# Four unused tiles in SBUF that shift where TensorE's operands begin

## The chip, the cores and the metric

The kernel runs on one core of one Trainium2 chip. The metric is device time in microseconds, taken over one execution of the whole program; the median of several runs is given. PE is TensorE, DVE VectorE, ACT ScalarE, POOL GpSimd, SP the queue that issues the DMAs.

## The reference

An attention layer over 12480 tokens of 128 channels with 32 inducing points, then two feed-forward layers of width 2048. Cut to what matters:

```python
def mab(q, kv):
    s = scale * (q @ kv.transpose(0, 2, 1))
    a = np.exp(s - s.max(-1, keepdims=True))
    a /= a.sum(-1, keepdims=True) + 1e-09
    return a @ kv
h = mab(I, x)                              # 32 inducing points look at all tokens
x = mab(x, h)                              # all tokens look at the 32 results
x = (s * np.maximum(x @ w_in, 0) ** 2 + b) @ w_out
y = x @ w_in2
g = np.where(y >= 1, y, np.where(y <= -1, 0.0, (y + 1) ** 2 / 4))
return g @ w_out2
```

## The kernel before

The tokens are cut into 25 blocks of 512 (the last has 192). A first stage of some 50 us loads x in seven groups of blocks, transposes the blocks on PE (L301), keeps a running softmax for the inducing points (L318, L363, L374) and ends with hT. A second stage starts the feed-forward work while the weights are still being turned into the form in which they are used; there the second matrix of the first layer is multiplied as plain fp32 (`out1_whole`, L721), and each of these matmuls stands in the trace as two records.

From about 125 us on the work goes in steps. A step is two chunks of 128 hidden units of one block, eight steps are a block, and each step does four things on PE, 20 matmuls with 512 columns each, all of type fp32r: two matmuls of the first layer's input side (L656, in1), six of the second layer's output side (L709 to L711, out2), six of the second layer's input side (L746 to L748, in2) and six of the first layer's output side (L709 to L711 again, out1). The six are three products for each of two chunks, since weights and activations are each split into a high part and a rest (hi, lo) to keep the accuracy of fp32. The stages of one step belong to different blocks: the second layer runs 18 steps behind the first. Between the matmuls ACT does relu, squares and one of the two casts, POOL the split behind the first layer (L235, L686), DVE the clip, the sum and the other rest (L753, L764, L774). The order of the steady part is written out in a list (ORDER), that of the start and the end comes from a planner with a table of durations. None of this uses addresses.

Addresses come from pools. A pool lays its tiles one behind the other in each of the 128 partitions. From the left of the memory come `keep` (ident, hT and five columns of one element, each taking 32 bytes), `xts` (x, later also y and cl), `homes` (six halves of the weights of 8192 bytes each, before that the loaded blocks xc), and then `pre` for the first stage, whose place is taken over by `wk` (g1, qin, hw, qt) at the `switch` of L541. From the right come `cv` (the weights being converted, win, wo_s), whose place is later taken over by `wk2` (hi, lo, o). The tile y of a block is held in a place of `xts`, hi and lo in `wk2`, the weights in `homes`. Because of the five small columns on the left, and of where the right side begins, all of the tiles that the matmuls of a step read begin 32 bytes beside a multiple of 64 in the built program. The starts in bytes of a partition, and their rest by 2048:

| tile | read by | before | rest | after | rest |
|---|---|---|---|---|---|
| x, y (first) | L746 to L748 | 17696 | 1312 | 18432 | 0 |
| halves (first) | weights of L709 to L711, L746 to L748 | 67616 | 32 | 69632 | 0 |
| qt | L656 | 143968 | 608 | 147456 | 0 |
| hw | weights of L656 | 141920 | 608 | 145408 | 0 |
| hi, lo (first) | L709 to L711 | 188384 | 2016 | 186368 | 0 |
| g1 | L721 | 117344 | 608 | 120832 | 0 |
| wo_s | weights of L721 | 182240 | 2016 | 180224 | 0 |

Of the kernel before, what the change touches and what calls it, by code (L numbers as in the profile page):

```python
# [10 lines left out]
F32 = mybir.dt.float32  # L11
# [85 lines left out]
def tb(bl):  # L97
    return TB if bl < NB - 1 else TBL
# [73 lines left out]
def moe_attn_kernel(ctx: ExitStack, tc: tile.TileContext, x, ind, w_in, w_out, s, b, w_in2, w_out2, out):  # L172
# [6 lines left out]
    def kt(shape, name, dt=F32):  # L179
        return keep.tile(shape, dt, tag=name, name=name)  # L180

    ident = kt([128, 128], "ident")
    xts = ctx.enter_context(tc.tile_pool(name="xts", bufs=1, reuse_waits="tile"))
    xT = []
    while len(xT) < NB:
        i = len(xT)
        pair = i in PAIRS
        t = xts.tile([C, 1 + pair, tb(i)], F32, tag=f"x{i}", name=f"x{i}")
        xT += [t[:, k, :] for k in range(1 + pair)]
    hT = kt([C, 4 * NM], "hT")  # L190
    bcol = kt([C, 1], "bcol")
    s_sb = kt([128, 1], "s_sb")
    b_sb = kt([128, 1], "b_sb")
    mhalf = kt([128, 1], "mhalf")
    mneg = kt([128, 1], "mneg")

    flat = lambda t: t.rearrange("p f d -> p (f d)")

# [9 lines left out]
        return halves[name, k]  # L208

    cx, px = ExitStack(), ExitStack()  # L210
    cv = cx.enter_context(tc.tile_pool(name="cv", bufs=1, side="right"))
    pb = cx.enter_context(tc.tile_pool(name="pb", bufs=1, space=PSUM, side="right"))
    pre = px.enter_context(tc.tile_pool(name="pre", bufs=1))
# [325 lines left out]
    pool = {}  # L539

    def switch():  # L541
        px.close()
        pool["wk"] = ctx.enter_context(tc.tile_pool(name="wk", bufs=1, reuse_waits="tile"))
        pool["pm"] = ctx.enter_context(tc.tile_pool(name="pm", bufs=1, space=PSUM, reuse_waits="tile"))

    def finish():
        t = add("PE", 0.12, f_pm, P["top", NG - 1], P["xT", NB - 1])
        t = add("DVE", 0.6, f_gm, t)
        t = add("PE", 0.05, f_pg, t)
        t = add("DVE", 0.13, f_w, t)  # L550
        tw = add("ACT", 0.1, lambda: nc.scalar.activation(w_, w_, AF.Exp, scale=scale), t)
        weighted(NG - 1)
        t = add("DVE", 0.07, lambda: nc.vector.tensor_mul(lsum, lsum, w_), tw, P["lsum", NG - 1])
        t = add("PE", 0.05, f_pl, t)
        t = add("DVE", 0.27, f_ri, t)
        t = add("DVE", 0.26, lambda: nc.vector.tensor_scalar(hsum, hsum, w_, ri, op0=ALU.mult, op1=ALU.mult),
                t, tw, P["hs", NG - 1])
        t = add("PE", 0.22, f_ht, t)
        t = add("DVE", 0.2, lambda: nc.vector.tensor_copy(hT, T.pop("pht")[:, :128]), t)
        P["hT"] = add("switch", 0.01, switch, t)  # L560
# [639 lines left out]
```

## Time and profile before

| | |
|---|---|
| runs | 1002.73, 999.62, 1002.39 us; median 1002.39 |
| profiled execution, span from first to last instruction | 999.5 us |
| PE busy | 977.5 us (98%) |
| ACT, DVE, POOL busy | 845.5, 806.1, 753.8 us |
| DMA, mean over the span | 28 GB/s |

The page of the profile gives busy time by engine and in 40 slices, with the clock that was granted to TensorE; the trace answers with waits (who waited for whom), windows (busy time in a stretch) and a timeline, in which the start of each instruction is read. For PE the starts matter: matmuls are pipelined, so one begins before the one ahead of it has ended, and durations overlap.

### The profile page before, as it was taken

How to read it: one execution, taken by the hardware profiler on the slowest of the kernel's cores; microseconds unless marked ns; L12 is line 12 of the kernel's file. 1: busy time of each engine (PE TensorE's matmuls, PEld its weight loads, DVE VectorE, ACT ScalarE, POOL GpSimd, SP SyncE). 2: the span in 40 equal slices, each digit the busy share in tenths (PEclk: the TensorE clock that was granted, in tenths of full speed). 3: DMA queues.
4: the chain of work that ended last, by engine and by line, in shares of the span. 5: the costliest groups of instructions: out<-in, count | busy, mean ns of one | idle time of the engine just before them, and what ended most of it. 6: DMA issues, size and time to landing. Idle time of an engine off the chain costs nothing.

```text
span 999.5 us, 12391 instructions
## 1 busy us (share of the span) xinstructions
PE 977.5 (98%) x4492; PEld 772.6 (77%) x4492; DVE 806.1 (81%) x834; ACT 845.5 (85%) x910; POOL 753.8 (75%) x510
## 2 busy tenths in 40 slices
PE   5999999999999999999999999999999999999997
PEld 3754588888888888888888888888888888888776
DVE  6868788888888878888788888878878878878895
ACT  5748989889898988998888898998998988898774
POOL 0121379888889888889889888888888888887463
PEclk9979999999999999999999999999999999999999
DMA  8602000100002000002000002000001000000001
GB/s 312 220 27 80 0 1 11 45 9 11 5 6 53 11 1 11 11 1 53 11 1 11 11 0 54 11 1 11 11 1 42 11 1 11 16 1 11 11 12 15
DMA packets 65469, 28.11 MB, mean 28 GB/s; under 512 B 54016, under 2 KB 58368, under 8 KB 65408
## 3 DMA queue, kind: packets, MB, share of 16 engines
q1 hardware_dynamic: 65408, 27.33, 11.2%
q8 instruction: 35, 0.57, 0.2%
q14 instruction: 26, 0.21, 0.1%
HBM read 14.80 MB, written 6.39 MB: 21 GB/s over the span
## 4 chain that ended last, share of the span: by engine, by line
PE 94%; DVE 2%; ACT 2%; DMA 1%; issue 0%; SPq 0%; ACTq 0%
PE y L709 17%; PE y L710 17%; PE y L711 17%; PE h L746 9%; PE h L748 9%; PE h L747 9%; PE h L656 9%; PE y L721 3%; PE ptr L301 1%; DMA xc<-in_x_dram 1%; ACT g L676 1%; DVE cl L753 1%; PE ph L374 1%; ACT g L669 1%; DVE lo L774 1%; PE pw L878 1%
## 5 line engine op out<-in xcount | busy, mean ns | idle before, releaser
L686 POOL TENSOR_TENSOR lo<-g,hi 128x1024 fp32r<-128x1024 f32 (+1 forms) x182 | 427.8, 2351 | 15.2
L753 DVE TENSOR_SCALAR cl<-h 128x1024 f32<-128x1024 f32 (+2 forms) x202 | 239.5, 1187 | 141.9 <-PE h L748 141.7
L757 ACT ACTIVATE cl<-cl,mhalf 128x1024 f32<-128x1024 f32 (+2 forms) x202 | 227.0, 1125 | 97.9 <-DVE cl L753 96.5
L709 PE MATMUL y<-hi,wout 128*128 128x512 f32 (+1 forms) x748 | 293.0, 392 | 0.9 <-DVE o L799 0.9
L710 PE MATMUL y<-lo,wout 128*128 128x512 f32 (+1 forms) x748 | 293.0, 392 | 0.0
L711 PE MATMUL y<-hi,wout 128*128 128x512 f32 (+1 forms) x748 | 292.8, 391 | 0.0
L235 POOL TENSOR_SCALAR hi<-g 128x1024 fp32r<-128x1024 f32 (+1 forms) x182 | 186.4, 1024 | 103.3 <-PE y L711 86.4
L764 DVE SCALAR_TENSOR_TENSOR h<-h,cl 128x1024 f32<-128x1024 f32 x182 | 223.4, 1227 | 14.0 <-ACT cl L757 2.7
L774 DVE TENSOR_TENSOR lo<-h,hi 128x1024 fp32r<-128x1024 f32 x182 | 221.3, 1216 | 1.2 <-ACT hi L231 0.5
L676 ACT ACTIVATE g<-g 128x1024 f32<-128x1024 f32 (+1 forms) x200 | 207.5, 1039 | 5.4
L669 ACT ACTIVATE g<-h 128x1024 f32<-128x1024 f32 (+1 forms) x197 | 194.3, 986 | 5.3 <-PE h L656 5.3
L231 ACT CAST hi<-h 128x1024 fp32r<-128x1024 f32 x182 | 181.8, 999 | 4.8 <-DVE h L764 4.8
L711 PEld LDWEIGHTS y<-hi,wout 128*128 128x128 f32 x748 | 140.6, 188 | 32.1
L710 PEld LDWEIGHTS y<-lo,wout 128*128 128x128 f32 x748 | 140.6, 188 | 31.8
L709 PEld LDWEIGHTS y<-hi,wout 128*128 128x128 f32 x748 | 140.6, 188 | 30.8 <-issue 1.3
L746 PE MATMUL h<-y,win 128*128 128x512 f32 (+1 forms) x400 | 156.2, 390 | 1.1 <-DVE lo L774 1.0
L748 PE MATMUL h<-y,win 128*128 128x512 f32 (+1 forms) x400 | 155.9, 390 | 0.0
L747 PE MATMUL h<-y,win 128*128 128x512 f32 (+1 forms) x400 | 153.7, 384 | 0.0
L656 PE MATMUL h<-qt,hw 128*128 128x512 f32 (+1 forms) x400 | 125.3, 397 | 0.7 <-ACT g L669 0.6
L656 PEld LDWEIGHTS h<-qt,hw 128*128 128x128 f32 x400 | 74.4, 188 | 24.1 <-issue 6.2
L746 PEld LDWEIGHTS h<-y,win 128*128 128x128 f32 x400 | 75.1, 188 | 19.8 <-DVE lo L774 2.0
L747 PEld LDWEIGHTS h<-y,win 128*128 128x128 f32 x400 | 75.2, 188 | 17.1
(139 smaller groups left out, 617.3 us busy)
## 6 DMA issues: line engine op xcount, KB each, us to landing
xc<-in_x_dram SPq DMA_DIRECT2D x24, 256.0 KB, 6.8
out_dram<-o SPq DMA_DIRECT2D x96, 64.0 KB, 2.2
qin<-x SPq DMA_DIRECT2D x92, 64.0 KB, 2.0
raw_in<-in_moe_w_in_dram SPq DMA_DIRECT2D x8, 512.0 KB, 5.8
raw_out<-in_moe_w_out_dram SPq DMA_DIRECT2D x8, 512.0 KB, 6.8
xc<-in_x_dram SPq DMA_DIRECT2D x1, 96.0 KB, 6.9
qin<-x SPq DMA_DIRECT2D x4, 24.0 KB, 2.7
out_dram<-o SPq DMA_DIRECT2D x4, 24.0 KB, 1.9
```

The costliest lines, as they stand in the source:

```text
L656: nc.tensor.matmul(p[:, j, :tb(bl)], hw[f // 4][:, (f % 4) * 128:(f % 4 + 1) * 128], qt[bl], start=True, stop=True)
L686: engine[eng].tensor_sub(lo1[t], g1.pop(t), hi1[t].bitcast(F32))
L709: nc.tensor.matmul(p, whi, hi[:, j, :], start=first, stop=False)
L710: nc.tensor.matmul(p, whi, lo[:, j, :], start=False, stop=False)
L711: nc.tensor.matmul(p, wlo, hi[:, j, :], start=False, stop=last)
L746: nc.tensor.matmul(p[:, j, :tb(bl)], whi, y1h[bl], start=True, stop=False)
L747: nc.tensor.matmul(p[:, j, :tb(bl)], wlo, y1h[bl], start=False, stop=False)
L748: nc.tensor.matmul(p[:, j, :tb(bl)], whi, y1l[bl], start=False, stop=True)
L753: nc.vector.tensor_scalar(cl[t][:, part(js)], h2[t][:, part(js), :tb(t // SPB)], -1.0, 1.0, op0=ALU.max, op1=ALU.min)
L757: nc.scalar.activation(k, k, AF.Square, bias=mhalf, scale=0.5)
L764: nc.vector.scalar_tensor_tensor(oo[t][:, part(js)], h, -1.0, cl[t][:, part(js)], op0=ALU.max, op1=ALU.add)
L774: engine[eng].tensor_sub(lo2[t][:, part(js)], oo[t][:, part(js)], hi2[t][:, part(js)].bitcast(F32))
```

## The change

Four tiles are allocated that nothing writes or reads: 736 bytes at the end of `keep`, 1280 bytes at the end of `xts`, 1472 bytes at the start of `wk`, and 2016 bytes at the right edge, in a pool of its own ahead of `cv`. All tiles laid out behind them shift; the table above has the starts before and after. The tiles of `keep` itself stay (ident at 16512, hT at 17024). The smaller tiles of `pre` that lie behind odd sizes (ind_sb, iT, hsum, e, eT and the last block of xc) were at multiples of 64 and are now 32 bytes beside one.

```diff
+    xts.tile([128, 320], F32, tag="xgap", name="xgap")
     hT = kt([C, 4 * NM], "hT")
...
     mneg = kt([128, 1], "mneg")
+    kt([128, 184], "gap")
...
     cx, px = ExitStack(), ExitStack()
+    right = ctx.enter_context(tc.tile_pool(name="right", bufs=1, side="right"))
+    right.tile([128, 504], F32, tag="rgap", name="rgap")
     cv = cx.enter_context(tc.tile_pool(name="cv", bufs=1, side="right"))
...
     def switch():
         px.close()
         pool["wk"] = ctx.enter_context(tc.tile_pool(name="wk", bufs=1, reuse_waits="tile"))
+        pool["wk"].tile([128, 368], F32, tag="wgap", name="wgap")
```

The instructions of all five queues are the same and in the same order. Since `wk` takes over the place of `pre` and the two shift by different amounts, a tile of `wk` may lie on other tiles of `pre` than before, and with that three waits differ, all in the start. On ACT, around 57 to 72 us, where the high parts of the first weights (hh) are cast and the first relus run, before:

```order
L882 CAST hh0_783<-pw0_768 128x512 [waits PE_49]
L882 CAST hh1_794<-pw1_781 128x512 [waits PE_49,Activation_49]
L882 CAST hh2_832<-pw2_823 128x512 [waits PE_49]
L669 ACTIVATE g1_0_844<-h1_0_838 128x1024 [waits PE_49]
L676 ACTIVATE g1_0_844<-g1_0_844 128x1024 [waits Activation_49]
L882 CAST hh3_862<-pw3_854 128x512 [waits PE_49]
L433 ACTIVATE cvs_out21_864<-raw_out21_581 128x512 [waits DMAHW7_49,DVE_49]
L606 ACTIVATE x1_65<-x1_65 128x512 [waits DVE_49]
L669 ACTIVATE g1_1_879<-h1_1_870 128x1024 [waits PE_49]
```

and the same place after the change:

```order
L887 CAST hh0_790<-pw0_775 128x512 [waits PE_49,Activation_49]
L887 CAST hh1_801<-pw1_788 128x512 [waits PE_49]
L887 CAST hh2_839<-pw2_830 128x512 [waits PE_49]
L674 ACTIVATE g1_0_851<-h1_0_845 128x1024 [waits PE_49]
L681 ACTIVATE g1_0_851<-g1_0_851 128x1024 [waits Activation_49]
L887 CAST hh3_869<-pw3_861 128x512 [waits PE_49]
L437 ACTIVATE cvs_out21_871<-raw_out21_587 128x512 [waits DMAHW7_49,DVE_49]
L611 ACTIVATE x1_65<-x1_65 128x512 [waits DVE_49]
L674 ACTIVATE g1_1_886<-h1_1_877 128x1024 [waits DMAHW2_49,PE_49]
```

Nothing moved here; the wait for ACT's own queue goes from hh1 to hh0, and the relu of step 1 waits for a DMA too. The third is on SP, where the first of the four DMAs that fill qin2 waits for PE before and not after.

## Rows read from the trace of the kernel before

**Rows 1.** The page: busy by engine, slices of PE and clock, chain.

```profile
PE 977.5 (98%) x4492; PEld 772.6 (77%) x4492; DVE 806.1 (81%) x834; ACT 845.5 (85%) x910; POOL 753.8 (75%) x510
...
PE   5999999999999999999999999999999999999997
...
PEclk9979999999999999999999999999999999999999
...
PE 94%; DVE 2%; ACT 2%; DMA 1%; issue 0%; SPq 0%; ACTq 0%
```

**Rows 2.** Waits, 125 to 910 us: who <- for whom: us, times, longest.

```profile
DVE cl L753 <- PE h L748: 134.8, 166, 0.9
POOL hi L235 <- PE y L711: 81.7, 94, 1.2
ACT cl L757 <- DVE cl L753: 79.6, 143, 0.6
```

**Rows 3.** Windows of 200 us: busy time by engine, sum and mean.

```profile
400.00:600.00 200.00, 200.00 (x868) 162.59 (x867) 163.08 (x146) 178.91 (x182) 178.19 (x118) 1.00 0.07 12
...
sum 600.00, PE 600.00 PEld 487.75 DVE 489.41 ACT 534.33 POOL 523.99; mean PE 200.00 PEld 162.58 DVE 163.14 ACT 178.11 POOL 174.66
```

**Rows 4.** Timeline of PE: start, duration; steps at 126, 500, 911 us.

```profile
125.72 0.62 PE L656 MATMUL h<-qt,hw 128*128 128x512 f32 x2
...
499.94 0.62 PE L656 MATMUL h<-qt,hw 128*128 128x512 f32 x2
500.39 0.39 PE L709 MATMUL y<-hi,wout 128*128 128x512 f32 x1
...
501.78 0.39 PE L746 MATMUL h<-y,win 128*128 128x512 f32 x1
...
503.16 0.39 PE L709 MATMUL y<-hi,wout 128*128 128x512 f32 x1
503.39 0.40 PE L710 MATMUL y<-lo,wout 128*128 128x512 f32 x1
503.63 0.39 PE L711 MATMUL y<-hi,wout 128*128 128x512 f32 x1
...
504.56 0.62 PE L656 MATMUL h<-qt,hw 128*128 128x512 f32 x2
...
911.12 0.39 PE L656 MATMUL h<-qt,hw 128*128 128x512 f32 x1
```

**Rows 5.** Timeline of PE in the start: third and sixth record of eight.

```profile
89.05 0.59 PE L721 MATMUL y<-g,wo_s 128*128 128x512 f32 x1
...
90.33 0.59 PE L721 MATMUL y<-g,wo_s 128*128 128x512 f32 x1
```

**Rows 6.** Groups of PE by shape: count, busy, mean ns of one.

```profile
L709 PE MATMUL y<-hi,wout 128*128 128x512 f32 x732 | 288.8, 395 | 0.9 <-DVE o L799 0.9
L710 PE MATMUL y<-lo,wout 128*128 128x512 f32 x732 | 288.6, 394 | 0.0
...
L748 PE MATMUL h<-y,win 128*128 128x512 f32 x384 | 151.5, 395 | 0.0
L746 PE MATMUL h<-y,win 128*128 128x512 f32 x384 | 151.5, 395 | 1.1 <-DVE lo L774 1.0
...
L656 PE MATMUL h<-qt,hw 128*128 128x512 f32 x384 | 122.3, 402 | 0.7 <-ACT g L669 0.6
...
L374 PE MATMUL ph<-xc,eT 128*32 128x128 f32 x192 | 6.5, 276 | 0.0
...
L363 PE MATMUL pe<-ident,e 128*128 128x128 f32 x24 | 3.9, 283 | 0.0
```

**Rows 7.** ACT's timeline at 71 us; xc's loads: issue times, time to landing.

```profile
71.18 1.02 ACT L669 ACTIVATE g<-h 128x1024 f32<-128x1024 f32 x1 [0.58 <-PE h L656]
...
L284 SPq DMA_DIRECT2D xc<-in_x_dram x25: 327/328/777, 3.0 to 26.9; - x25
...
xc<-in_x_dram SPq DMA_DIRECT2D x1, 96.0 KB, 6.9
```

## The prediction

> **What bounds the kernel now.** I read the profile from the whole towards the single instruction. First the busy line and the slices [rows 1]: PE is busy for 977.5 of 999.5 us, at nine tenths in all slices but the first and the last, with the granted clock at its upper level of 2.4 GHz almost throughout, and the chain that ended last runs 94% over PE. Then the waits between 125 and 910 us [rows 2]: the longest are DVE's, POOL's and ACT's, DVE and POOL both for matmuls of PE, and no row has PE as the one that waits. So in four fifths of the run nothing that another engine does sets the time. The windows say the same [rows 3]: in 600 us PE is busy for 600.00, ACT for 534.33, POOL for 523.99, DVE for 489.41.
>
> What is left is how fast PE itself streams. A busy PE is not a PE at its peak, so I look at starts, not at durations, which overlap. One steady step is 20 matmuls of 512 columns of fp32r, and it goes from 499.94 to 504.56 us [rows 4]: 4.62 us, or 231.0 ns for a matmul. The same row is at 125.72 and at 911.12 us [rows 4], 785.40 us apart, which is 170 steps of 4.62 us: 3400 matmuls at one pace, whatever the softmax steps, stores and loads in between do. For comparison, the plain fp32 matmuls of the start (L721, two records each): three records take from 89.05 to 90.33 us [rows 5], 0.427 us a record. At 2.4 GHz that is 1024 cycles, two for each of 512 columns, with nothing on top; half of it, 213.3 ns, is the time of 512 columns at one a cycle. An fp32r matmul takes 17.7 ns more, 8%. That excess is the only time in the steady part that a change of addresses could give back.
>
> **The change part by part.** No instruction is added or taken away, and on PE, DVE and POOL the order and the waits are the same as before. Only addresses move, and three waits.
>
> *Excess per matmul.* All tiles that the fp32r matmuls read (qt, hw, hi, lo, y, the halves) start 32 bytes beside a multiple of 64 before and at a multiple of 2048 after. There are 3 x 732 + 4 x 384 = 3732 such matmuls of 512 columns [rows 6]; L711 and L747, not shown there, have as many as their neighbours. The trace of before has none of them with another start, so their price is bounded from both sides. If the whole excess is due to the start, 17.7 ns x 3732 = 66 us go. If none is, nothing goes. Between them: 2048 bytes that begin in the middle of a 64-byte piece touch 33 pieces, not 32; if a matmul took time by pieces it would fall from 231.0 to 224.0 ns, and 7.0 ns x 3732 = 26 us would go. Upward, the largest step that the order of starts shows is 503.39 to 503.63 us [rows 4], about 5 ns over the mean; if all 3400 steady matmuls became so, 17 us would come.
>
> I take zero, by the rows nearest to it. The fp32 records of L721 read g and wo_s, which also start 32 beside a multiple of 64, and show no excess at all [rows 5]; so such a start costs nothing where columns are read at half the pace. That does not exclude a cost at the full pace, but nothing in the trace shows one. Nor does the offset that a tile has within 2048 bytes: within the step, the two matmuls of L656 (moving tile at offset 608) take 0.45 us, the six of L709 to L711 behind them (offset 2016) 1.39 us, the six of L746 to L748 (offset 1312) 1.38 us and the last six 1.40 us [rows 4], that is 225, 232, 230 and 233 ns each. Four places with three offsets lie within 4% and the same offset gives 232 and 233, so I see a pace of fp32r, not a cost of a place.
>
> The Trainium skill, "SBUF — State Buffer", Specifications (TRN2), gives the memory lines of 16 bytes; a start 32 beside a multiple of 64 is the start of such a line as much as one at a multiple of 2048, and by that the sum is zero. No run here shows the line's size.
>
> *Other readers of the moved tiles.* If DVE, ACT or POOL became slower or faster by the move, PE would cover it: the steady step leaves ACT 4.62 - 4.62 x 534.33 / 600 = 0.51 us and POOL 0.59 us [rows 3]. If that cover went (a PE step of 4.27 us, all of the excess gone), ACT would still need only 4.11 us, and so would be late next, but just short of setting the pace.
>
> *Tiles that lose their start.* In the first 50 us, e, eT, hsum, iT and ind_sb go from multiples of 64 to 32 beside one. They are read as fp32, which at that start shows no excess [rows 5]: zero. The most of them are the 192 and 24 of L374 and L363 [rows 6]; if each paid 17.7 ns, 4 us would be added.
>
> *Waits.* ACT's relu into the second g1 buffer (L669) now also waits for the landing of the last xc block, since its buffer lies where that tile was. The last xc load was issued at 26.9 us and took 6.9 us to land [rows 7]; the relu starts at 71.18 us [rows 7]. The wait was over some 37 us before, and nothing queued behind it on ACT is held. A CAST of hh waits for an earlier instruction of ACT's own queue in place of its neighbour, and the first qin2 DMA on SP waits for PE no more; it stands behind qin1 in the same queue, so at most its own short wait goes. All zero.
>
> The sum is zero. The profiled execution's span is 999.5 us, 0.1 below the fastest of the runs shown and 2.9 below their median of 1002.4; zero against the span is zero against the median, and I give 1002.
>
> **The rivals.** *The start does cost at the full pace (faster).* For it: the excess is there, it is the same in all 170 steps, and all tiles of fp32r share the start. Against it: the fp32 records without excess, and that the trace names no cause. Worked out above: 976 us by pieces of 64 bytes, 936 us if all goes. Since ACT's 4.11 us a step stays under PE's 4.27, no other engine takes the gain back in the steady part.
> The Trainium skill, "TensorE: Matmul & The Clock Gate", Back-to-back issue gap, speaks for this rival: it gives a matmul of N columns N / 2.4 + 2.5 ns, 215.8 ns for 512. The steady step disagrees with its 231.0 ns, and if the start were the reason, 15.2 ns x 3732 = 57 us would go, an estimate from that page of 946 us.
>
> *Weights and moving data from the same place (slower).* After the change both of PE's streams begin at multiples of 512 bytes in all matmuls. If the weight load, which runs beside the stream of the matmul before, met it more often, each steady matmul would go to the largest step seen, 5 ns more: 1002 + 17 = 1019 us. It decides from 1 ns a matmul (3.7 us) on. Against it: hw and qt already stand at equal offsets (608, steps of 512), and L656 has the shortest steps of all [rows 4].
>
> *The change doesn't do what it says.* The addresses of the built program do move, so this is left only for the few tiles of the first 50 us named above, at most 4 us.
>
> **How the numbers follow.** No change: 0.50. Faster through the start: 0.38, of which 0.12 for about 976 us or a little above, 0.26 for deeper, down to 936. Slower: 0.12, most of it up to 1019. A measurement of this kernel tells about 0.3% (3 us) from no change. The range goes down to 945, where seven eighths of the excess are gone (58 of 66 us), so that only the lowest part of the faster rival is left out, and up to 1006, the 4 us of the first stage; some 0.15 lies outside. The likeliest case's own range is 999 to 1006.
>
> **What would show it.** Right: the step in the timeline is again 4.62 us, and L721's records 0.427 us. Wrong, faster: the step is 4.48 us or less with PE still at 100% in the windows; if it is 4.27 to 4.35, look whether ACT then shows as the one that PE waits for. Wrong, slower: a step above 4.64 us with the same set of waits. If the step is unchanged and the time is not, the first 120 us or the end have moved, and the waits of ACT and SP in the start are the place to look. What would make the prediction wrong is one thing above all: that fp32r's 8% over one column a cycle is a matter of where a tile begins and not of the type.

## The result and the profile after

The changed kernel takes 986.01 us (median of 4 runs, 984.17 to 987.54); beside it the kernel before took 1002.56 us (999.62 to 1006.63). The ratio is 0.983, with a 95% interval of 0.980 to 0.986: faster by 1.7%. I had forecast no change, so the likeliest case was wrong; the time lies inside the stated range, 945 to 1006 us. The profiled execution took 984.17 us with a span of 982.4 us, 17.1 us less than the span of before.

The page of the changed kernel: busy time by engine, and the chain that ended last.

```profile
PE 959.7 (98%) x4492; PEld 770.0 (78%) x4492; DVE 805.0 (82%) x834; ACT 843.6 (86%) x910; POOL 753.3 (77%) x510
...
PE 93%; ACT 2%; DVE 2%; DMA 2%; issue 0%; DVEq 0%; ACTq 0%
```

Against [rows 1] the counts are the same on every engine. PE's busy time fell by 17.8 us, that of the others by 3 us or less, and the chain still runs over PE. So PE does the same work faster. Where it does shows in its timeline (start, duration): the steps that answer to those of [rows 4], lines moved by five.

```profile
123.89 0.39 PE L661 MATMUL h<-qt,hw 128*128 128x512 f32 x1
...
500.16 0.62 PE L661 MATMUL h<-qt,hw 128*128 128x512 f32 x2
500.61 0.39 PE L714 MATMUL y<-hi,wout 128*128 128x512 f32 x1
...
501.97 0.39 PE L751 MATMUL h<-y,win 128*128 128x512 f32 x1
...
503.33 0.39 PE L714 MATMUL y<-hi,wout 128*128 128x512 f32 x1
503.56 0.39 PE L715 MATMUL y<-lo,wout 128*128 128x512 f32 x1
503.78 0.39 PE L716 MATMUL y<-hi,wout 128*128 128x512 f32 x1
...
504.69 0.61 PE L661 MATMUL h<-qt,hw 128*128 128x512 f32 x2
...
894.56 0.39 PE L661 MATMUL h<-qt,hw 128*128 128x512 f32 x1
```

A step goes from 500.16 to 504.69: 4.53 us, where it was 4.62 [rows 4]. The 170 steps go from 123.89 to 894.56, in 770.67 us in place of 785.40: 4.533 us each, **226.67 ns a matmul in place of 231.0**. That is 14.7 us of the 17.1. The mean is not the only thing that changed: by the single starts in the trace, those of a step were 224 to 236 ns apart before, and now every one is 226 or 227. Two matmuls in 0.45 us, six in 1.36, six in 1.36: all places of the step have one pace.

The first steady step comes 1.8 us earlier (123.89 for 125.72). One stretch holds most of that, 50 to 60 us. Its window in the kernel before (columns as in [rows 3]: span, busy time and count of PE, PEld, DVE, ACT, POOL, granted clock, DMA share, GB/s):

```profile
50.00:60.00 10.00, 9.59 (x32) 7.23 (x33) 6.07 (x19) 2.50 (x6) 2.54 (x2) 0.51 0.01 2
```

and in the changed kernel:

```profile
50.00:60.00 10.00, 9.62 (x46) 7.48 (x47) 5.86 (x19) 2.53 (x5) 2.52 (x2) 0.66 0.01 2
```

The granted clock is at 1.2 GHz for nearly all of these 10 us before (0.51) and for about two thirds after (0.66). Ahead of them, from 48 to 50 us, it is at 2.4 GHz (1.00) in both, while PE is busy for 0.93 us before and 1.08 us after. About 3 us fewer at half speed are worth 1.5 us, an estimate. Whether the change does that is not shown: of the kernels below some have about the one value (e3, e8) and some the other (e1, e2, e5, e6), without regard to their pace. The remaining 0.5 us lies behind the last of the 170 steps.

### The profile page after: what moved, and what is told of

Read it like the earlier page. It is cut to its first block, busy times and chain, and to the rows that moved or that the text cites. A ratio compares the mean times of both kernels' runs of the same rounds, so it can differ in the third digit from the quotient of the medians.

```text
span 982.4 us, 12391 instructions
## 1 busy us (share of the span) xinstructions
PE 959.7 (98%) x4492; PEld 770.0 (78%) x4492; DVE 805.0 (82%) x834; ACT 843.6 (86%) x910; POOL 753.3 (77%) x510
## 4 chain that ended last, share of the span: by engine, by line
PE 93%; ACT 2%; DVE 2%; DMA 2%; issue 0%; DVEq 0%; ACTq 0%
PE y L714 17%; PE y L715 17%; PE y L716 17%; PE h L751 9%; PE h L753 9%; PE h L752 9%; PE h L661 9%; PE y L726 3%; DMA xc<-in_x_dram 1%; PE ptr L305 1%; DVE cl L758 1%; ACT g L681 1%; PE ph L378 1%; ACT g L674 1%; DVE lo L779 1%; PE pw L883 1%
## 5 line engine op out<-in xcount | busy, mean ns | idle before, releaser
L762 ACT ACTIVATE cl<-cl,mhalf 128x1024 f32<-128x1024 f32 (+2 forms) x202 | 226.8, 1124 | 83.9 <-DVE cl L758 83.6
L714 PE MATMUL y<-hi,wout 128*128 128x512 f32 (+1 forms) x748 | 289.5, 387 | 0.9 <-DVE o L804 0.9
L715 PE MATMUL y<-lo,wout 128*128 128x512 f32 (+1 forms) x748 | 289.3, 387 | 0.0
L716 PE MATMUL y<-hi,wout 128*128 128x512 f32 (+1 forms) x748 | 289.2, 387 | 0.0
L751 PEld LDWEIGHTS h<-y,win 128*128 128x128 f32 x400 | 75.1, 188 | 17.8 <-DVE lo L779 2.0
```

Of the source, the lines that this page charges most:

```text
L714: nc.tensor.matmul(p, whi, hi[:, j, :], start=first, stop=False)
L715: nc.tensor.matmul(p, whi, lo[:, j, :], start=False, stop=False)
L716: nc.tensor.matmul(p, wlo, hi[:, j, :], start=False, stop=last)
L751: nc.tensor.matmul(p[:, j, :tb(bl)], whi, y1h[bl], start=True, stop=False)
L762: nc.scalar.activation(k, k, AF.Square, bias=mhalf, scale=0.5)
```

## The experiments

Every matmul has two operands in SBUF: the *moving* one, whose 512 columns are streamed, and the *weights*, which are loaded (PEld in the profile) beside the stream of another matmul. The table gathers the starts of the tiles modulo 256 bytes in all full kernels that ran, with the mean steady step and the ratio to the kernel before on the same chip (the changed kernel's is that of the section above). In the first product of a step (L656) qt moves over hw; in the others hi, lo or y moves over the halves. The letters of the theories are those of the expectations.

| kernel | qt, hw | hi, lo | y | halves | step, us | ratio, 95% |
|---|---|---|---|---|---|---|
| before | 96 | 224 | 32 | 32 | 4.620 | |
| changed | 0 | 0 | 0 | 0 | 4.533 | 0.983 [0.980, 0.986] |
| e1_by64 | 128 | 192 | 64 | 64 | 4.613 | 0.996 [0.994, 0.998] |
| e2_halves32 | 0 | 0 | 0 | 32 | 4.660 | 1.005 [1.003, 1.008] |
| e3_hilo32 | 0 | 224 | 0 | 0 | 4.627 | 0.999 [0.997, 1.000] |
| e5_same256 | 32 | 32 | 32 | 32 | 4.533 | 0.983 [0.981, 0.985] |
| e6_right256 | 96 | 32 | 32 | 32 | 4.587 | 0.992 [0.990, 0.994] |
| e8_wk256 | 32 | 224 | 32 | 32 | 4.633 | 0.999 [0.998, 1.000] |

### Is it the start beside a multiple of 64? (e1, e2, e3)

Three kernels take back parts of the change. e1 leaves all starts at multiples of 64, but no longer of 2048:

```diff
-    xts.tile([128, 320], F32, tag="xgap", name="xgap")
-    kt([128, 184], "gap")
+    kt([128, 8], "gap")
-    right.tile([128, 504], F32, tag="rgap", name="rgap")
+    right.tile([128, 8], F32, tag="rgap", name="rgap")
-        pool["wk"].tile([128, 368], F32, tag="wgap", name="wgap")
```

> All tiles that the changed kernel moved to multiples of 2048 bytes begin at a multiple of 64 here, none of those behind the odd sizes at a multiple of 2048 (rests 1344, 640, 1984, 64): only 32 bytes are added on the left and 32 on the right. Theory A, the 32 bytes beside a multiple of 64 were the cost: the steady step is 4.533 us as in the changed kernel and the time is within 3 us of 986. Theory B, a larger unit (256, 512 or 2048 bytes) matters: the step stays near 4.62 us and the time near 1002.

e2 moves only the halves 32 bytes off, e3 only the right side, in the steps hi and lo:

```diff
-    xts.tile([128, 320], F32, tag="xgap", name="xgap")
+    xts.tile([128, 328], F32, tag="xgap", name="xgap")
-        pool["wk"].tile([128, 368], F32, tag="wgap", name="wgap")
+        pool["wk"].tile([128, 360], F32, tag="wgap", name="wgap")
```

> The changed kernel with the six weight halves alone 32 bytes beside a multiple of 64; everything that streams (qt, hi, lo, y) stays at multiples of 2048. 18 of the 20 matmuls of a step read such weights. Theory A1, the streamed operand's start costs: step 4.533 us, time 986. Theory A2, the weights' start costs: 18 of 20 matmuls pay the whole 4.33 ns, step 4.611 us, time near 1000. Theory A3, it is the place of the two against each other that costs: a step above 4.533 too, perhaps above 4.62.

```diff
-    right.tile([128, 504], F32, tag="rgap", name="rgap")
+    right.tile([128, 512], F32, tag="rgap", name="rgap")
```

> The changed kernel with the right side alone shifted: hi and lo, the streamed operands of the 12 matmuls of out1 and out2, are 32 bytes beside a multiple of 64; the weights, qt and y stay at multiples of 2048. Theory A1, the streamed operand's start costs: 12 of 20 pay 4.33 ns, step 4.585 us, time about 995; the six matmuls of in2 stay at 226.7 ns each. Theory A2, the weights' start: step 4.533 us, time 986.

One step in PE's timeline, of e1, where it takes 4.61 us:

```profile
502.11 0.63 PE L659 MATMUL h<-qt,hw 128*128 128x512 f32 x2
...
506.72 0.63 PE L659 MATMUL h<-qt,hw 128*128 128x512 f32 x2
```

of e2, 4.66 us:

```profile
502.06 0.62 PE L661 MATMUL h<-qt,hw 128*128 128x512 f32 x2
...
506.72 0.62 PE L661 MATMUL h<-qt,hw 128*128 128x512 f32 x2
```

and of e3, 4.63 us:

```profile
500.13 0.63 PE L661 MATMUL h<-qt,hw 128*128 128x512 f32 x2
...
504.76 0.63 PE L661 MATMUL h<-qt,hw 128*128 128x512 f32 x2
```

e1 settles that the 64 is not the point: with every start at a multiple of 64 it gains 7 of the 87 ns that the change gains in a step. Over 170 steps that is 1.2 us; of the 3.3 us by which its span is shorter than that of the kernel before (996.2 and 999.5), another 1.9 lie ahead of the first steady step, which comes at 123.81 us. So its ratio of 0.996 is for the larger part not the steady pace. e2 settles that a place by itself isn't either: only the halves stand off, as they did before, and the step is *slower* than before. In e3 it is as slow as before with hi and lo alone displaced. What the three have in common is products whose moving operand and weights stand at different rests of 256.

### The same with PE alone (e4)

One kernel has nothing but series of 48 matmuls, back to back, and leaves out all of the reference. Its core, where m0 and w0 are the starts of the moving operand and the weights from multiples of 2048 bytes:

```diff
+    for k, (name, t, m0, w0, n, m) in enumerate(SERIES):
+        m_, w_ = mv[t]
+        p = ps.tile([128, 512], F32, tag=f"p{k % 4}", name=name)
+        for _ in range(N if t != "f" else N // 4):
+            nc.tensor.matmul(p[:m, :n], w_[:, w0:w0 + m], m_[:, m0:m0 + n], start=True, stop=True)
```

> Only series of equal matmuls on TensorE, 48 of a kind one behind the other, with nothing else running; nothing of the reference is computed and the output is zeros. A warm-up, then fp32r with 512 columns: the streamed operand starts at 0, 4, 8, 16, 32, 48, 64, 96, 128, 256, 1024 bytes beside a multiple of 2048 (aa to ak), the weights at 4, 16, 32, 64, 512 (ba to be), both (ca 32 and 32, cb 32 and 64, cc 96 and 32), fewer columns (da, db 256; dc, dd 384; at 0 and 32), fewer weight columns (ea, eb 64; ec, ed 32; at 0 and 32), bf16 (fa, fb), fp32 (ga, gb, 12 matmuls of two records), and the first two again (ha, hb). Theory A1: 226.7 ns in aa, ag, ai, aj, ak and in all of ba to be, about 231 where the streamed start is no multiple of 64. Theory A2: 226.7 in all of aa to ak, about 231 in ba, bb, bc. If other engines' reading took part, all series would show 226.7 or less. For the 226.7 ns that stay in the changed kernel (13.3 ns over 512 columns at one a cycle): if it is the weight load beside the stream, ea and ec fall below 226.7; if it is the type, they stay and fa shows 216; fp32 shows 2 x 429 ns per matmul at either start.

PE's timeline of it, one row a series; the difference of two neighbouring starts, divided by 48, is the pace (the first matmuls of a series carry a little of the one ahead).

```profile
18.33 11.04 PE L59 MATMUL aa<-mr,wr 128*128 128x512 f32 x48
29.21 11.52 PE L59 MATMUL ab<-mr,wr 128*128 128x512 f32 x48
...
62.88 11.36 PE L59 MATMUL ae<-mr,wr 128*128 128x512 f32 x48
74.08 11.35 PE L59 MATMUL af<-mr,wr 128*128 128x512 f32 x48
...
118.66 11.07 PE L59 MATMUL aj<-mr,wr 128*128 128x512 f32 x48
129.56 11.05 PE L59 MATMUL ak<-mr,wr 128*128 128x512 f32 x48
...
151.61 11.36 PE L59 MATMUL bb<-mr,wr 128*128 128x512 f32 x48
162.81 11.35 PE L59 MATMUL bc<-mr,wr 128*128 128x512 f32 x48
174.00 11.36 PE L59 MATMUL bd<-mr,wr 128*128 128x512 f32 x48
...
196.11 11.08 PE L59 MATMUL ca<-mr,wr 128*128 128x512 f32 x48
207.02 11.36 PE L59 MATMUL cb<-mr,wr 128*128 128x512 f32 x48
218.22 11.15 PE L59 MATMUL cc<-mr,wr 128*128 128x512 f32 x48
...
301.66 10.53 PE L59 MATMUL fa<-mb,wb 128*128 128x512 bf16 x48
312.03 10.52 PE L59 MATMUL fb<-mb,wb 128*128 128x512 bf16 x48
322.39 10.46 PE L59 MATMUL ga<-mf,wf 128*128 128x512 f32 x24
```

- aa, both at 0: (29.21 - 18.33) / 48 = 226.7 ns, the changed kernel's pace, with no other engine at work. ae, moving at 32: 233.3. bc, weights at 32: 233.1.
- **ca, both at 32: 227.3, and 226.8 beyond its first six gaps.** cb, moving at 32 and weights at 64: 233.3. So an equal start is as good as a start at 2048, and it is the distance of the two that costs. cc, moving at 96 and weights at 32, has 228.9 and so has ag, moving at 64 and weights at 0: the same distance, 64, and the same pace.
- aj, moving at 256: 227.1 by the rows, 226.66 beyond the first six. The distance counts modulo 256 bytes.
- fa and fb, bf16 with the moving operand at 0 and at 32: 216.0 and 215.8 by the rows, 215.83 beyond the first six for both. fp32 (ga, gb): 429.1 ns a record for both, beyond the first six. Neither feels the distance.

With this theories A1 and A2 fell, by which one operand's own start costs: ae displaces the one, bc the other, and both are slow. What stands is A3 of e2's expectation, the place of the two against each other. In its sharper form it is called C: the pace of an fp32r matmul depends on the distance of the start of its moving operand from that of its weights, modulo 256 bytes; at 0 it is 226.7 ns, wherever both begin.

### Put to the test in the kernel (e5, e6)

C says that two tiles of 192 bytes do all that the change does, with every start still 32 beside a multiple of 64. e5 is the kernel before with these:

```diff
+    right = ctx.enter_context(tc.tile_pool(name="right", bufs=1, side="right"))
+    right.tile([128, 48], F32, tag="rgap", name="rgap")
...
+        pool["wk"].tile([128, 48], F32, tag="wgap", name="wgap")
```

> The kernel before with two unused tiles of 192 bytes, one at the right edge and one at the start of wk. All starts stay 32 bytes beside a multiple of 64, but now all of them leave the same rest by 256 (32). Theory C, formed from the series: what costs is the distance between the start of the streamed operand and the start of the weights that are loaded beside it, taken by 256 bytes; it is 0 in all matmuls here. So the steady step is 4.533 us as in the changed kernel, and the time 984 to 988. Theory A, the place of a tile by itself: nothing gained over the kernel before, 4.62 us and about 1002.

e6 has the first two lines alone, so that qt and hw stay at a rest of 96:

> The kernel before with one unused tile of 192 bytes at the right edge, which moves hi, lo, o (and win, wo_s in the start) and nothing else. Then hi and lo leave the same rest by 256 as the weight halves (32), y did so already, and qt and hw (96) still differ from the halves by 64. Theory C, with the weights of the next matmul as those that are loaded beside a stream: 18 of 20 at 226.7 ns, the second matmul of L656 at 228.9 (distance 64) and the last of out1 at 233.4 (distance 192, by the series with the weights at 64): step 4.542 us, up to 4.56 if neighbours are drawn in; time 986 to 992. Theory A: 4.62 us and about 1002.

One step in PE's timeline, of e5:

```profile
500.97 0.62 PE L659 MATMUL h<-qt,hw 128*128 128x512 f32 x2
...
505.51 0.62 PE L659 MATMUL h<-qt,hw 128*128 128x512 f32 x2
```

and of e6:

```profile
501.43 0.62 PE L658 MATMUL h<-qt,hw 128*128 128x512 f32 x2
...
506.01 0.62 PE L658 MATMUL h<-qt,hw 128*128 128x512 f32 x2
```

e5 has the changed kernel's step, 4.53 us, and its ratio, 0.983, at 985.06 us. Theory C holds, and the change's multiples of 2048 are not needed. e6 is between the two, but its 4.587 us a step and its 994.65 us lie above what I expected (4.56 and 992 at most): all its own distances are 0, hw and qt included, and yet the six matmuls of the second product (hi, lo) go at 231.7 ns. So it is not each matmul's own pair alone.

### What the neighbours do (e7, e8, e9)

e7 repeats the series at finer distances and alternates pairs; e8 is e6's counterpart, with only the last line of e5's diff; e9 has series of 120 matmuls, in which the distances change after each matmul as in the kernels' steps, or once for a single matmul. For e9 the diff to e4's loop is

```diff
-        for _ in range(N if t != "f" else N // 4):
+        for i in range(N if t != "f" else N // 4):
+            m0, w0 = at[i % len(at)]
```

> Only series of 48 equal matmuls on TensorE again, nothing of the reference computed, output zeros. aa to aq: the streamed operand at 0 to 256 bytes in steps of 16 beside a multiple of 2048, ar at 384, as at 512, the weights at 0. Theory C: aa, aq and as 226.7 ns, ae (64) 228.9, the others up to 233. ba to bd: both at 4, 16, 64, 160 bytes: 226.7 by theory C, above it where a start by itself counts. ca and cb tell which weights count: in ca the matmuls alternate between (0, 0) and (32, 32), so that each has distance 0 from its own weights and 32 from those of the next; in cb between (0, 32) and (32, 0), the other way round. If the weights of the next matmul count: ca about 233, cb 226.7; if its own: ca 226.7, cb about 233. cc and cd are the same with 128. da to df: 192, 320, 448 columns at distance 0 and 32: if the 13.3 ns that stay are a fixed cost, 146.7 ns for 320 and 200.0 for 448 at distance 0 (for 192 the weight load bounds at about 112). ea, eb: weights of 96 and 64 columns. ga, gb: fp32, 429 ns a record at either distance.

> The kernel before with one unused tile of 192 bytes at the start of wk, which moves g1, qin, hw, qt, qf and y1f alone: qt and hw now leave the rest 32 by 256, as the halves and y do; hi and lo keep the rest 224, distance 192 to the halves. Theory C with each matmul paying for its own distance: 12 of 20 at 233.4, 8 at 226.7, step 4.614 us, about 1001. Theory D, a wrong distance also unsettles the matmuls behind it (in the kernel with the right side moved, 18 matmuls of distance 0 went at 229 on average): the eight are drawn up too, step 4.62 to 4.67 us, 1002 to 1011.

> Series of 120 matmuls of fp32r with 512 columns on TensorE, nothing else running, nothing of the reference computed, output zeros. ca repeats the 20 distances of a steady step of the kernel before, cb that of the kernel with the right side moved, cc that with wk moved, cd that with both. If the pace of the kernels is a matter of TensorE's own two streams and of no other engine, the series go at 231.0, 229.3, the same as the run beside this one, and 226.7 ns. ba and bb: (0, 0) throughout with a single matmul at a distance of 32 after twenty, once by the streamed operand, once by the weights; theory D: more than the one or two matmuls beside it leave 226.7 ns, some twelve as in the kernel with the right side moved; without carry-over two at most. bc: (0, 0) and then (32, 32) for good, which is distance 0 again. da and db: weights, or streamed operand, alternate between 0 and 32: 230.0 if half of the matmuls pay 6.7 ns, about 233 if all do.

e7, moving operand displaced in steps of 16 bytes, mean pace in ns beyond the first six gaps: 0: 226.7; 16: 231.6; 32: 233.3; 48: 233.4; 64: 228.8; 80: 231.2; 96: 233.4; 112: 231.3; 128: 232.5; 144: 233.3; 160: 234.2; 176: 233.3; 192: 233.4; 208: 234.6; 224: 233.4; 240: 226.7; 256: 226.9. Besides 0 only 240 is as good, which C didn't foresee, and it isn't the distance that does it: e4's bb, with the weights at 16 and the moving operand at 0, is 240 apart too, and has 233.3 ns. Where both begin at the same 4 or 16 bytes the pace is 237.7 and 231.2, so at starts that are no multiple of 32 the place itself counts as well. At multiples of 32, C's rule holds within 1 ns in every series of equal matmuls of 512 columns with 128 weight columns. The rows of e7's timeline that these readings use, where the difference of two neighbouring starts, divided by 48, is again the pace:

```profile
185.78 11.05 PE L63 MATMUL ap<-mr,wr 128*128 128x512 f32 x48
196.67 11.08 PE L63 MATMUL aq<-mr,wr 128*128 128x512 f32 x48
...
229.68 11.57 PE L63 MATMUL ba<-mr,wr 128*128 128x512 f32 x48
241.09 11.26 PE L63 MATMUL bb<-mr,wr 128*128 128x512 f32 x48
252.19 11.09 PE L63 MATMUL bc<-mr,wr 128*128 128x512 f32 x48
...
274.04 11.28 PE L63 MATMUL ca<-mr,wr 128*128 128x512 f32 x48
285.17 11.20 PE L63 MATMUL cb<-mr,wr 128*128 128x512 f32 x48
296.20 11.12 PE L63 MATMUL cc<-mr,wr 128*128 128x512 f32 x48
```

The series ca and cb, which were to tell a matmul's own weights from the next one's, fit neither (231.8 and 230.0 beyond the first six).

e8's step is 4.64 us in the rows below and 4.633 in the mean, within what I expected of carry-over (4.62 to 4.67) and above the 4.614 of each matmul paying for itself. The time, 1002.23 us, can't tell the two apart.

```profile
500.33 0.62 PE L657 MATMUL h<-qt,hw 128*128 128x512 f32 x2
...
504.97 0.62 PE L657 MATMUL h<-qt,hw 128*128 128x512 f32 x2
```

PE's timeline of e9; here a difference of starts divided by 120 is the pace.

```profile
144.53 27.88 PE L65 MATMUL ca<-mr,wr 128*128 128x512 f32 x120
...
172.25 27.68 PE L65 MATMUL cb<-mr,wr 128*128 128x512 f32 x120
...
199.77 27.96 PE L65 MATMUL cc<-mr,wr 128*128 128x512 f32 x120
...
227.56 27.39 PE L65 MATMUL cd<-mr,wr 128*128 128x512 f32 x120
...
254.79 27.76 PE L65 MATMUL da<-mr,wr 128*128 128x512 f32 x120
```

- ca, with the distances of the kernel before: 231.0 ns. cb, those of e6: 229.3; in the kernel 4.587 us / 20 = 229.3. cc, those of e8: 231.6; in the kernel 4.633 / 20 = 231.7. cd, those of e5: 226.9, and 226.67 behind its first five. da, with weights that alternate between 0 and 32 under a moving operand at 0: 230.0 from start to start. db, with the moving operand alternating instead: 231.7.
- Even the single gaps agree. ca's 20 are 226 229 229 225 236 231 236 231 228 229 234 235 225 230 232 236 231 236 230 231 ns; the kernel before, by place in the step over its steady steps, has 226 229 228 226 236 231 236 231 228 229 233 236 224 231 232 236 231 236 231 231.
- One matmul whose moving operand is off by 32, in a series at distance 0: the gaps from there are 235 233 233 236 224 231 236 228 233 231, and then 226 and 227 again. One wrong distance draws in ten gaps, its own among them. One whose weights are off draws in four, 235 229 232 231, and the first of them lies in front of this matmul, where its weights are loaded beside the stream of the one ahead.
- bc has (0, 0) for twenty matmuls and then (32, 32) for good. Every matmul's own distance is 0, but eight gaps are disturbed, 235 230 224 231 236 228 233 231, and again the first lies in front of the first displaced matmul. Both point to the weights of the next matmul as those that a stream meets. That is not all, as e7's cb shows: there the next weights always begin where the stream does, and it goes at 230.0 ns and not at 226.7.

So PE's two streams alone make the kernel's pace, in the kernel before down to 1 ns in each gap, and what other engines do in SBUF has no part in it. The carry-over fits e6: its two matmuls of L656 lie at 96 between neighbours at 32, and their own two gaps and the ten behind them are disturbed. How the two streams hinder each other, and why the trouble lasts so long, is not shown.

For Trainium2 the Trainium skill, "TensorE: Matmul & The Clock Gate", Step-by-step: what each phase is for, says that loading the next weights takes no read bandwidth of SBUF from the running matmul, as PE has two independent read ports. For bf16 and fp32 no series here speaks against it; for fp32r the 226.7 and 233.4 ns do: the distance between the two streams is all that differs. That they meet in SBUF's reads, and not behind them, is not shown.

## Where the prediction was right and where it was wrong

**What bounds the kernel: right.** PE's pace over 170 equal steps, and no wait of PE. The pace went down and the time followed: 3400 matmuls x 4.33 ns = 14.7 us of the 17.1. The rest lies outside the 170 steps, most of it in the stretch of the changed clock. Behind PE nothing was late; the others waited less. The waits of the changed kernel from 125 to 890 us (us in total, times, longest), which answer to [rows 2]:

```profile
DVE cl L758 <- PE h L753: 118.1, 164, 0.9
POOL hi L239 <- PE y L716: 67.7, 74, 1.1
ACT cl L762 <- DVE cl L758: 66.9, 142, 0.5
```

and the sum of its windows from 200 to 800 us, which answers to [rows 3]:

```profile
sum 600.00, PE 600.00 PEld 496.82 DVE 498.00 ACT 542.75 POOL 532.49; mean PE 200.00 PEld 165.61 DVE 166.00 ACT 180.92 POOL 177.50
```

All three sums of waits fell by 12 to 17%, in a stretch 3% shorter, and ACT's need is 4.533 x 542.75 / 600 = 4.10 us a step, as the 4.11 worked out before: the moved addresses did nothing to the other engines.

**Excess per matmul, "I take zero": the step that failed.** It was 4.33 ns, a quarter of the 17.7, and below the 7.0 that pieces of 64 bytes would have given. That 986 us lies within the range is luck: the range reached down to 945 for a start that costs by itself, which the runs rule out for starts at multiples of 32, and a step of 4.53 us stands under none of the signs that I had listed (4.62, 4.48 or less, above 4.64). Two readings led to the zero.

- *The fp32 records.* They are not quite without excess: by the single starts a record takes 429 ns, before and after, some 2.4 over 1024 cycles; the rows of [rows 5], to 10 ns, hid that. "Such a start costs nothing where columns are read at half the pace" was right all the same, and still is (below), but it doesn't carry over: e4's fp32 series feel no distance at all where its fp32r series do. I had written that it doesn't exclude a cost at full pace, and then took the row for the nearest all the same.
- *"I see a pace of fp32r, not a cost of a place."* I compared the offsets of the moving tiles alone (608, 2016, 1312) and found no order in 225, 232, 230 and 233 ns. The quantity was the distance to the weights, which no row of a matmul shows; and the carry-over of up to ten matmuls, in steps of 20, mixes what each place pays. The unevenness of 224 to 236 ns in one and the same instruction was the sign: work of one shape that waits for nothing could have had one pace, as these matmuls have at distance 0. I had the widest of these gaps in hand (236 ns by the single starts; the rows shown give 240), and used it only to bound a loss.

The line of 16 bytes that the Trainium skill gives in "SBUF — State Buffer", Specifications (TRN2), and from which I worked out zero, didn't tell it either: a displacement by two such lines costs 6.7 ns (aa and ae).

**The rival "the start does cost" had the sign, not the reason.** e1 gains 0.4%, little of it in the steps, with every start at a multiple of 64, and e5 all of the gain with none. Its price, 26 us or more, was too high as well: 226.67 ns, still 13.3 over 512 columns at one a cycle, stays at any start that I tried. The series give 119.9 ns for 256 columns, 146.7 for 320, 173.3 for 384: each of these, too, is 13.3 ns over one column a cycle; 448 columns, at 202.7, are 16.0 over it. bf16's 215.83 ns are 2.5 over it. That agrees with the gap formula of the Trainium skill, "TensorE: Matmul & The Clock Gate", Back-to-back issue gap, but not with the about 131 ns that the same section gives for a stream of matmuls with weight loads; fp32r follows neither. Fewer weight columns don't take the 13.3 away (64 columns: 230.0 ns). What it is stays open.

**The rival "weights and moving data from the same place" named the two streams that matter, with the wrong sign.** Equal starts are the best case. Its counter-evidence, that L656 has equal offsets and the shortest steps, fits the mechanism, but weakly: in e3 and e8, where qt and hw are equal too, the same two matmuls take 229 and 235, and 225 and 235 ns, since what runs ahead of them carries over. I read it only as a reason that nothing gets worse.

**The rest: right.** The fp32 matmuls of the start, and ACT's relu with its added wait, in the changed kernel's timelines of PE and ACT:

```profile
86.81 1.02 PE L726 MATMUL y<-g,wo_s 128*128 128x512 f32 x2
...
88.10 1.02 PE L726 MATMUL y<-g,wo_s 128*128 128x512 f32 x2
```

```profile
69.36 1.02 ACT L674 ACTIVATE g<-h 128x1024 f32<-128x1024 f32 x1 [0.58 <-PE h L661]
```

Three records take 1.29 us, against 1.28 in [rows 5], the same 429 ns a record but for the rounding; the relu waits 0.58 us for PE, as in [rows 7], and for no load. The 4 us set aside for tiles that lose their start were not needed: the stretch before the first steady step grew shorter.

## What to carry over

Where TensorE runs fp32r matmuls with a weight load beside each, lay out the tiles so that the starts of moving operand and weights are multiples of 32 bytes and agree modulo 256, with one rest for neighbouring products too; two unused tiles of 192 bytes were worth 1.7% here. This is shown for 512 columns and 128 weight columns. Where equal instructions that wait for nothing have unequal gaps, ask what they meet in passing: look at both operands, and at the instructions around it, before calling the mean a property of the type. A disputed cost of one engine is measured best in a kernel of that engine alone; here it gave back the full kernel's pace to 0.1 ns.

## What the runs showed of the hardware

- fp32r, 512 columns, weights of 128 columns loaded beside: 226.67 ns at starts that are equal modulo 256 bytes and multiples of 32, 229 to 235 with the moving operand displaced by 16 to 224, without order; 226.7 again with it displaced by 240, but 233.3 with the weights displaced by 16 (e4, e7).
- One matmul at a wrong distance disturbs up to ten gaps, its own and those behind it. One change of the common start of both operands, at distance 0 throughout, disturbs eight (e9).
- Equal starts that are no multiple of 32 bytes cost: 237.7 ns at 4 bytes, 231.2 at 16 (e7).
- Of the lengths tried, the distance costs only those of 448 and 512 columns: at 448 columns 206.7 ns with the moving operand off by 32 against 202.7 with none, at 384 173.3 for both, at 320 146.6 against 146.7, at 256 even 117.8 against 119.9 (e4, e7).
